# Re-cutting the first strip's output products around a batch's attention work, and moving one kv block by half a slot

## The chip, the cores and the metric

The kernel runs on one core of a Trainium2 chip. The metric is the time of one execution on the device in microseconds (us), the median of several executions. A profile is the record of one execution; times inside it count from the first recorded instruction ("span"), and the span is some 1.8 us shorter than the time. All runs here are fast ones at a granted TensorE clock of 0.998 to 1.000; the two single looks (b_again1, b_again2) have no state of their own but the same clock. Each time is compared with the kernel before in the same rounds.

## The reference

Linear attention over 8 batches, 8 heads, 576 tokens and head size 64, with a normalisation per head and token, then a bilinear feed-forward layer:

```python
kv = np.einsum('bhsd,bhse->bhde', k, v)
out = np.einsum('bhsd,bhde->bhse', q, kv)
rms = np.sqrt(np.mean(out * out, axis=-1, keepdims=True) + 1e-06)
x = out / rms * g_norm            # to 4608 tokens x 512
y = ((x @ w_a) * (x @ w_b)) @ w_out   # 512 -> 1536 -> 512
```

## The kernel before

The feed-forward layer goes over nine strips of 512 tokens. In each strip, 12 units (L161 with wa_t, wb_t) make the hidden block `ab`, and 4 groups of 12 products with wo_t make the output. A product is one matmul of the algorithm, and a bank is one of the eight parts (0 to 7) of the memory P that TensorE writes its results into. TensorE is the scarce engine (98% busy), so the attention of later batches is slipped between these products. Batch 1 is slipped between the output products of strip 0, one head pair p per step:

```python
    ffn_o(0, 0, X[0])                     # group 0: 12 products, bank 4
    pieces = [(1, h1), (1, h2), (2, h1), (2, h2), (3, h1), (3, h2)]
    for n, (g, fcs) in enumerate(pieces):
        halves[0] = n > 0                 # from n=1 each product is two 64-column halves
        o_mm(0, g, O, fcs)                # 6 products of group g into bank O = 3
        if fcs is h2:
            o_out(0, g, O)                # copy of bank 3 to SBUF (VectorE or ScalarE), store
        if 0 <= n - 2 < NP:
            A.pss(n - 2, SS)              # sums of squares (TensorE), rs = 1/sqrt (ScalarE)
            A.pst(n - 2, X[n % 2])        # xt = x * g * rs (VectorE)
        if 0 <= n - 1 < NP:
            A.x(n - 1, X[(n - 1) % 2])    # x = q @ kv; needs kvb and qT; banks 4,5 or 0,1
            A.psq(n - 1, X[(n - 1) % 2])  # square (ScalarE)
        if n < NP:
            A.qtr(n, 2)                   # q transposes into bank 2; needs the load of qt
            A.kv1(n, 2)                   # kv products into bank 2; need the loads of kt, vt
            A.kv_out(n, P[:, 2, STRIP - D :])  # kvb: two copies (ScalarE)
            A.qtr_out(n, 2)               # qT: copy (VectorE)
```

Batch 2, the third batch when counted from 1, is slipped into strip 1. `slot(A, 1, n)` is called after unit n, and with n - 0.5 between a unit's two halves. At slot `k0` all 40 kv products of the batch run, the "kv block" (its loads are `ktl` and `vtl`, issued by GpSimd behind all others; the first 8 products read only the larger load of each, from the ninth on the small second load is read too); at slot `x0` come the token products (L293), which read their result `kvs`:

```python
        k0, x0 = {1: (5, 6.5), 2: (1, 2.5), ... }[s]
        if n == k0 and s in (1, 2, 3, 5):
            ...
                for p in range(NP):
                    a.kv(p, kb[:, i, p, :])
```

Cuts in this code are marked by "..."; the comments are mine.

## Time and profile before

| | kernel before |
|---|---|
| time, first 3 runs | 312.71, 312.70, 312.86 us |
| span of the profile | 310.8 us |
| TensorE busy | 98% |
| first output product (start) | 35.15 us |
| first unit of strip 1 (start) | 49.96 us |

The timelines that carry the argument stand in the prediction. Here is one more, of the weight loads (start, length, then engine, line, operation and count, and in brackets the idle time ahead of it). It shows how the wait of the third batch's kv block looks from the other side:

```profile
60.10 0.42 PEld L178 LDWEIGHTS <-ktl 128*64 128x64 bf16 x9
60.69 0.58 PEld L178 LDWEIGHTS <-ktl 128*64 128x64 bf16 x31 [0.17 <-issue]
```

Nine weights are in, the ninth product does not start, and the next weight load comes at 60.69. The view that sums up waits has no row that names the load (it has 0.2 us of "PEld L178 <- issue"); a start-to-start comparison finds the wait.

### The profile page before, as it was taken

How to read it: one execution, taken by the hardware profiler on the slowest of the kernel's cores; microseconds unless marked ns; L12 is line 12 of the kernel's file. 1: busy time of each engine (PE TensorE's matmuls, PEld its weight loads, DVE VectorE, ACT ScalarE, POOL GpSimd, SP SyncE). 2: the span in 40 equal slices, each digit the busy share in tenths (PEclk: the TensorE clock that was granted, in tenths of full speed). 3: DMA queues.
4: the chain of work that ended last, by engine and by line, in shares of the span. 5: the costliest groups of instructions: out<-in, count | busy, mean ns of one | idle time of the engine just before them, and what ended most of it. 6: DMA issues, size and time to landing. Idle time of an engine off the chain costs nothing.

```text
span 310.8 us, 6542 instructions
## 1 busy us (share of the span) xinstructions
PE 304.3 (98%) x2684; PEld 157.6 (51%) x2701; DVE 140.6 (45%) x235; ACT 117.0 (38%) x231; POOL 101.3 (33%) x123
## 2 busy tenths in 40 slices
PE   7899999999999999999999999999999999999996
PEld 3444476655555555555555555444444444444444
DVE  4544335458248603484386123752782143214321
ACT  3743255354255313551564034632651233123310
POOL 8954991093274630043646300221240000000000
PEclk9999999999999999999999999999999999999999
DMA  8999999999899999047998990073021200030002
GB/s 180 197 196 199 201 188 168 161 169 184 174 137 185 139 174 193 2 84 134 178 177 118 162 188 2 19 160 110 20 51 42 103 1 0 34 103 0 0 36 101
DMA packets 94403, 36.29 MB, mean 117 GB/s; under 512 B 64934, under 2 KB 89894, under 8 KB 94374
## 3 DMA queue, kind: packets, MB, share of 16 engines
q0 software_dynamic: 59120, 18.44, 56.6%
q1 hardware_dynamic: 34786, 16.93, 25.0%
q10 hardware_dynamic: 468, 0.51, 0.6%
q8 instruction: 21, 0.34, 0.5%
q14 instruction: 8, 0.07, 0.1%
HBM read 37.78 MB, written 12.98 MB: 163 GB/s over the span
## 4 chain that ended last, share of the span: by engine, by line
PE 79%; DMA 12%; POOL 7%; issue 1%; ACT 0%; POOLq 0%
PE P L161 77%; DMA wb_t<-in_moe_w_b_dram 6%; DMA vtl<-in_v_dram 4%; DMA wo_t<-in_moe_w_out_dram 2%; PE P L293 1%; PE P L178 1%; POOL vt L119 1%; POOL qt L119 1%; POOL qs L142 1%; POOL kt L119 1%; POOL wa_t L477 0%; POOL wb_t L477 0%; POOL wo_t L134 0%; POOL ktl L145 0%; POOL vtl L145 0%
## 5 line engine op out<-in xcount | busy, mean ns | idle before, releaser
L377 DVE TENSOR_TENSOR ab<-P,asb 128x512 bf16<-128x512 f32 x108 | 74.4, 691 | 103.2 <-PE P L161 99.9
L161 PE MATMUL P<-xt,wb_t 128*64 128x512 bf16 (+1 forms) x641 | 111.4, 379 | 0.2
L161 PE MATMUL P<-xt,wa_t 128*64 128x512 bf16 (+1 forms) x636 | 111.0, 379 | 0.6 <-issue 0.2
L373 ACT CAST asb<-P 128x512 bf16<-128x512 f32 x108 | 63.1, 586 | 89.6 <-PE P L161 89.5
L161 PE MATMUL P<-wo_t,ab 128*64 128x512 bf16 (+3 forms) x673 | 95.5, 371 | 0.3
L161 PEld LDWEIGHTS <-ab 128*64 128x64 bf16 (+1 forms) x678 | 47.5, 106 | 45.0
L161 PEld LDWEIGHTS <-wa_t 128*64 128x64 bf16 (+1 forms) x644 | 46.0, 106 | 46.2 <-issue 0.6
L161 PEld LDWEIGHTS <-wb_t 128*64 128x64 bf16 (+1 forms) x644 | 45.8, 106 | 45.8
L330 POOL TENSOR_TENSOR sqt<-rst,g_all 128x512 f32<-128x512 f32 (+1 forms) x24 | 25.0, 1046 | 83.0 <-ACT rst L323 83.0
L429 ACT COPY osb<-P 128x512 f32<-128x512 f32 x17 | 10.0, 586 | 70.2 <-PE P L161 60.2
L431 DVE COPY osb<-P 128x512 f32<-128x512 f32 x18 | 12.4, 691 | 44.9 <-PE P L161 40.4
L142 POOL DMA_DIRECT2D qs<-in_q_dram x12 | 19.8, 1654 | 0.7 <-issue 0.3
L314 DVE TENSOR_REDUCE sst<-sqt 128x8 f32<-128x512 f32 (+1 forms) x24 | 16.3, 680 | 1.7 <-ACT sqt L310 1.5
L339 DVE TENSOR_TENSOR qv<-P,sqt 128x512 bf16<-128x512 f32 x18 | 12.3, 681 | 0.0
L330 POOL TENSOR_TENSOR k_x<-rst,g_all 128x512 f32<-128x512 f32 x6 | 6.3, 1044 | 17.4 <-ACT rst L323 17.4
L323 ACT ACTIVATE rst<-sst,eps_t 128x8 f32<-128x8 f32 (+1 forms) x30 | 9.0, 300 | 7.2 <-DVE sst L314 7.0
L310 ACT ACTIVATE sqt<-P 128x512 f32<-128x512 f32 x18 | 10.5, 585 | 0.1
L243 DVE SCALAR_TENSOR_TENSOR xt<-P,g_col,rs 128x288 bf16<-128x288 f32 x16 | 7.5, 511 | 5.1 <-ACT rs L233 5.1
L134 POOL DMA_DIRECT2D wo_t<-in_moe_w_out_dram x12 | 6.4, 530 | 6.7 <-DMA wb_t<-in_moe_w_b_dram 3.2
L233 ACT ACTIVATE rs<-P,eps_t 128x576 f32<-128x576 f32 (+1 forms) x9 | 6.1, 689 | 3.7 <-PE P L161 3.4
L139 POOL COPY gate<-qT 1x1 bf16<-1x1 bf16 x5 | 0.9, 177 | 18.9 <-DVE kvs L618 14.0
L444 PE MATMUL P<-zeros 128*128 128x512 bf16 x16 | 5.8, 510 | 1.2 <-DVE eps_t L461 1.2
(72 smaller groups left out, 131.7 us busy)
## 6 DMA issues: line engine op xcount, KB each, us to landing
out_dram<-osb SPq DMA_DIRECT2D x23, 256.0 KB, 2.1
qs<-in_q_dram POOLq DMA_DIRECT2D x12, 288.0 KB, 7.5
ktl<-in_k_dram POOLq DMA_DIRECT2D x6, 512.0 KB, 9.6
vtl<-in_v_dram POOLq DMA_DIRECT2D x6, 512.0 KB, 12.2
out_dram<-osb SPq DMA_DIRECT2D x13, 128.0 KB, 2.4
wo_t<-in_moe_w_out_dram POOLq DMA_DIRECT2D x12, 128.0 KB, 6.0
wa_t<-in_moe_w_a_dram POOLq DMA_DIRECT2D x5, 256.0 KB, 8.9
wb_t<-in_moe_w_b_dram POOLq DMA_DIRECT2D x5, 256.0 KB, 9.5
```

The source lines that it names most:

```text
L119: nc.gpsimd.dma_start(out=t[:, hs, :, :], in_=src[b, hs].rearrange("h (t c) d -> t h c d", c=EC))
L142: nc.gpsimd.dma_start(out=d[:, hs, :], in_=q[b, hs].rearrange("h t d -> t h d"))
L161: nc.tensor.matmul(o[r], lhsT=lhsT[:, r], rhs=rhs, **kw)
L310: nc.scalar.activation(sqt[c % 3][r], self.by_head(c)[r], AF.Square)
L314: nc.vector.reduce_sum(sst[c % 3][r], sqt[c % 3][r].rearrange("t j p d -> t (j p) d"), axis=mybir.AxisListType.X,)
L323: nc.scalar.activation(rst[c % 3][r], sst[c % 3][r], AF.Abs_reciprocal_sqrt, bias=eps_t[r], scale=1.0 / D,)
L330: nc.gpsimd.tensor_mul(sqt[c % 3][r].rearrange("t j p d -> t (j p) d"), rst[c % 3][r].unsqueeze(2).to_broadcast([n, H, D]), g_all[r].unsqu ...
L339: nc.vector.tensor_mul(t[r].rearrange("t (p j) d -> t j p d", j=2), self.by_head(c)[r], sqt[c % 3][r])
L373: nc.scalar.copy(self.t, self.a)
L377: nc.vector.tensor_mul(abt[self.s % 2][self.fc], self.b, self.t)
L429: nc.scalar.copy(t, P[:, i, :])
L431: nc.vector.tensor_copy(t, P[:, i, :])
```

## The change

The intent is to let the kv products of pairs 0 and 1 come later, when their loads have landed, by putting two more output products ahead of them, and to do the same to the third batch's kv block with half a slot. The second group moves to bank 1, so that the third group's first two products can follow it at once. No work is added or removed; two more products run at full width and two fewer as halves.

```diff
-    h1, h2 = range(0, FC // 2), range(FC // 2, FC)
...
-    pieces = [(1, h1), (1, h2), (2, h1), (2, h2), (3, h1), (3, h2)]
-    for n, (g, fcs) in enumerate(pieces):
+    cuts = (12, 20, 26, 32, 36, 42, 48)
+    for n, cut in enumerate(cuts[1:]):
         halves[0] = n > 0
-        o_mm(0, g, O, fcs)
-        if fcs is h2:
-            o_out(0, g, O)
+        for i in range(cuts[n], cut):
+            g, fc = divmod(i, FC)
+            bank = X[1] + 1 if g == 1 else O
+            o_mm(0, g, bank, (fc,))
+            if fc == FC - 1:
+                o_out(0, g, bank)
...
-        k0, x0 = {1: (5, 6.5), 2: (1, 2.5), 3: (4, 5.5), ...}[s]
+        k0, x0 = {1: (5.5, 6.5), 2: (1, 2.5), 3: (4, 5.5), ...}[s]
```

More of the change, by code (lines that the diff above doesn't have):

```diff
@@ L608, in slot @@
             xs = tuple(x0 + x for x in (0, 1.5, 2.5, 4, 5))
-        k0, x0 = {1: (5, 6.5), 2: (1, 2.5), 3: (4, 5.5), 4: (0, 0.5), 5: (4, 5.5), 6: (0, 0.5)}[s]
+        k0, x0 = {1: (5.5, 6.5), 2: (1, 2.5), 3: (4, 5.5), 4: (0, 0.5), 5: (4, 5.5), 6: (0, 0.5)}[s]
         if n == k0 and s in (1, 2, 3, 5):
```

## The prediction

> **What bounds the kernel now.** I read the page first, then the chain that ended last, then the TensorE timeline around the two places that the diff touches, and last the weight-load, VectorE and ScalarE timelines at the spots where TensorE started late. The page says who is the bound:
>
> ```profile
> span 310.8 us, 6542 instructions
> PE 304.3 (98%) x2684; PEld 157.6 (51%) x2701; DVE 140.6 (45%) x235; ACT 117.0 (38%) x231; POOL 101.3 (33%) x123
> ```
>
> TensorE is busy 98% of the span at a granted clock of 1.000, and neither the amount nor the shape of its work changes, so the change can only be worth TensorE's own late starts. The chain of waits names where a transfer, not TensorE, set the pace:
>
> ```profile
> 36.47 0.63 POOL vt L119
> ...
> 47.20 13.45 DMA vtl<-in_v_dram
> 60.69 0.69 PE P L178 x32
> 61.38 2.59 PE P L161 x24
> ```
>
> Columns are start, length (us), what. The chain is one row of GpSimd loads up to the load of the third batch's v (vtl), then TensorE alone to the end: after 60.69 nothing but TensorE sets the time. So a microsecond saved on TensorE after 60.69 is a microsecond off the span, and one saved before counts only if the landing at about 60.65 does not take it back. The TensorE timeline (start, length, line, operands) shows the late starts:
>
> ```profile
> 39.13 0.45 PE L202 MATMUL P<-ident,qt 96*64 96x96 bf16 x12
> 39.60 0.38 PE L178 MATMUL P<-vt,kt 96*64 96x64 bf16 x12
> ...
> 41.33 0.45 PE L202 MATMUL P<-ident,qt 96*64 96x96 bf16 x12
> 41.82 0.38 PE L178 MATMUL P<-vt,kt 96*64 96x64 bf16 x12
> ...
> 43.80 0.45 PE L202 MATMUL P<-ident,qt 96*64 96x96 bf16 x12
> 44.05 0.38 PE L178 MATMUL P<-vt,kt 96*64 96x64 bf16 x12
> ...
> 45.54 0.44 PE L161 MATMUL P<-sq,ones 128*64 128x288 bf16 x4
> 45.92 0.44 PE L161 MATMUL P<-qT,kvb 128*64 128x288 bf16 x4
> ```
>
> The lengths are modelled and overlap, so read start to start. From the q transposes (L202) to the kv products (L178) it is 0.25 us undisturbed (43.80 to 44.05), but 0.47 for head pair 0 and 0.49 for pair 1. So these kv products start 0.22 and 0.24 us late; they wait for the pair's v load (issued 34.24 and 36.47; that group lands 5.3 to 5.9 us after issue, so about 39.6 and 41.8). From the sums of squares to the x product (kvb) it is 0.24 elsewhere (43.31 to 43.55), 0.38 here: 0.14 us late. A fourth late start is the kv block of the third batch:
>
> ```profile
> 60.32 1.07 PE L178 MATMUL P<-vtl,ktl 128*64 128x64 bf16 x40
> 61.19 1.06 PE L161 MATMUL P<-xt,wa_t 128*64 128x512 bf16 x8
> ...
> 86.20 0.80 PE L178 MATMUL P<-vtl,ktl 128*64 128x64 bf16 x40
> 86.83 1.03 PE L161 MATMUL P<-xt,wa_t 128*64 128x512 bf16 x8
> ```
>
> The same 40 products take 0.63 us at 86.20 and 0.87 at 60.32, so 0.24 us is waiting for vtl's landing. All four together are 0.22 + 0.24 + 0.14 + 0.24 = 0.84 us, 0.27% of the span: the ceiling of any gain.
>
> **What the Trainium skill says.** "TensorE: Matmul & The Clock Gate", Back-to-back issue gap, gives N/2.4 + 2.5 ns for one warm matmul, 216 ns at N=512; the trace agrees (the eight halves of four 512-column products take 0.86 us, 62.06 to 62.92). Part 3 of that page says that matmuls on different column tiles run at the same time; the trace agrees: twelve half-width products took 1.30 us (39.79 to 41.09), 216 ns a pair, as one full-width product. So doing two more products at full width and two fewer in halves costs nothing. "Perfetto Trace Analysis", Tensor Engine Instruction, says a recorded start lies after the semaphores are met and the end is computed; that is why I read waits as late starts. "PSUM — Partial Sum Buffer", PSUM bank collisions, says the scheduler orders two engines that touch one bank and quadrant even at different columns; the trace agrees: VectorE's copy of qT out of bank 2 always comes after ScalarE's kvb copies out of it.
>
> **The change, part by part.** It adds and removes no work. (a) Over the first strip's remaining 36 output products the cuts move from 6,6,6,6,6,6 to 8,6,6,4,6,6. Before the transposes of pairs 0, 1 and 2 stand two more products than before (2 x 0.216 = 0.43 us), before those of pair 3 as many as before. (b) The second group accumulates in bank 1 instead of 3, so the third group's first two products need not wait for the second's copy; before, about 1.3 us of other work lay between, and no wait shows there. (c) The third batch's kv block comes after the first half of unit 6 instead of before it: 4 x 0.216 = 0.865 us later in the stream.
>
> Step by step, from 35.15 where the output products start. Pair 0's transposes move from 39.13 to 39.56, its kv to 39.81, past the landing at 39.6: **0.22 us saved**. Then 6 products (1.30), x of pair 0 (0.24), transposes (0.25): pair 1's kv is due at 39.81 + 0.19 + 1.30 + 0.24 + 0.25 = 41.79, almost exactly the landing of 41.8. So the second stall goes too, **0.24 us saved**. But both savings together are only what the two extra products cost: TensorE is at 41.8 at the same point of the pair-1 step, only two products ahead.
>
> Here is the catch. Everything that follows pair 1's kv comes at its old time: six products, the sums for pair 0 at about 43.3, and behind them this chain:
>
> ```profile
> 44.56 0.94 DVE L243 SCALAR_TENSOR_TENSOR xt<-P,g_col,rs 128x288 bf16<-128x288 f32 x2 [1.30 <-ACT rs L233]
> 45.42 0.45 DVE L209 COPY qT<-P 128x576 bf16<-128x576 bf16 x1
> 45.79 0.68 DVE L431 COPY osb<-P 128x512 f32<-128x512 f32 x1
> ```
>
> Sums (43.31) to ScalarE rs (43.78, 0.74) to VectorE's two xt products (44.56) to qT of pair 2 (45.42 to 45.87); ScalarE's kvb copies, behind rs and sq, end at the same 45.38. TensorE's x of pair 2 started at 45.92, just after qT: this is the 0.14 us stall above. In the new order TensorE reaches it with 4 products instead of 6, 0.43 us sooner, and the chain is not sooner. So I expect x of pair 2 to start at about 45.9 again, now **0.55 us late instead of 0.14**: 0.43 is given back. After it both orders have done the same work (36 products), so TensorE is where it was, at best 0.03 us ahead. **Part (a) and (b): 0.22 + 0.24 - 0.43 = 0.03 us.** Two further places are close but hold: the third group's copy, on VectorE after qT, ends at 46.47 and the fourth group needs its bank at about 46.58; x of pair 3 still has six products ahead of it.
>
> Part (c): the kv block comes at 60.29 + 0.865 = 61.15 against a landing at 60.65, half a microsecond clear: **0.24 us saved**, and nothing takes it back, as TensorE runs without a late start of this kind from there to the end (later irregular spacings are 0.10 us at each batch's token products, in both kernels, and single missing records). The first user of its result, the token products at slot 6.5, comes 0.10 us (a change of tile shape) after 1.73 us of other products; VectorE's copy (0.42 us; after the kv block it started within 0.25) is done about 1.1 us ahead, and qT's transposing transfer (issued 50.5, 11.2 us to landing, 61.7) is 2 us ahead.
>
> Sum: 0.03 + 0.24 = about 0.26 us. 312.71 - 0.26 = **312.45 us**, 0.08% faster.
>
> **Rivals.** First, that the pieces' gain survives: if x of pair 2 does not wait for qT, or the chain moves up with the rest, 0.22 + 0.24 + 0.24 = 0.70 us come off, 312.0. For it: this is plainly what the cuts are for. Against it: VectorE runs from xt to qT without a gap and TensorE starts 0.05 us after qT ends. Second, that a new wait outgrows the gain: the shortened pair-2 slot lets the third group's copy or sq of pair 1 (ended 45.06, and the sums now due at 45.09) hold TensorE, or the late kv block leaves the token products waiting for kvs. The first two would cost about 0.1 us, the third is 1.1 us off; 312.6 to 312.8. Third, that the transfers land elsewhere than in the profiled execution: loads are one row at about 200 GB/s up to 60 us, so if vtl lands 0.5 us later in unprofiled runs, moving the block saves up to 0.7 us, 312.0; if it lands 0.3 us sooner, the whole change is worth nothing, 312.7.
>
> **Range and chances.** The three runs before lie within 0.16 us, so the range is set by the rivals: 312.1 to 312.75. The whole ceiling is 0.84 us and no new wait I can name reaches 1 us, against 6.25 us for 2%: faster 0.005, same 0.99, slower 0.005.
>
> **What would show it.** Right: kv of pair 0 some 0.25 us after its transposes; pair 1's near 41.8 with at most 0.05 us of waiting; x of pair 2 near 45.9 with 0.55 us of late start behind qT; the kv block of the third batch in 0.63 us; token products near 63.65. Wrong: x of pair 2 before 45.7 (first rival), sums of pair 1 or the fourth group's first product late (second), or the block still in pieces (third).

## The result

Over six runs each the kernel before took 312.60 us (312.23 to 312.86) and the changed one 312.59 us (312.39 to 312.73). The ratio is 1.0, with a 95% interval of 0.9987 to 1.0013. A ratio is the mean time of one kernel's runs over that of the other's of the same rounds, so it is not quite the ratio of the medians quoted.

The profile of the changed kernel, in the TensorE timeline at the places shown of before:

```profile
39.60 0.45 PE L202 MATMUL P<-ident,qt 96*64 96x96 bf16 x12
39.88 0.35 PE L178 MATMUL P<-vt,kt 96*64 96x64 bf16 x12
...
41.61 0.42 PE L202 MATMUL P<-ident,qt 96*64 96x96 bf16 x12
41.87 0.35 PE L178 MATMUL P<-vt,kt 96*64 96x64 bf16 x12
...
45.15 0.42 PE L161 MATMUL P<-sq,ones 128*64 128x288 bf16 x4
45.95 0.44 PE L161 MATMUL P<-qT,kvb 128*64 128x288 bf16 x4 [0.37 <-DVE qT L209]
...
61.21 0.82 PE L178 MATMUL P<-vtl,ktl 128*64 128x64 bf16 x40
61.84 1.06 PE L161 MATMUL P<-xt,wb_t 128*64 128x512 bf16 x8
```

The three load waits are gone: 0.28 and 0.26 us from transposes to kv products, 0.63 us for the kv block. In their place x of pair 2 starts 0.80 us after its sums where 0.24 is undisturbed: 0.56 us late, behind VectorE's qT copy. VectorE's timeline is here that of before, shifted by 0.02 us:

```profile
44.58 0.94 DVE L243 SCALAR_TENSOR_TENSOR xt<-P,g_col,rs 128x288 bf16<-128x288 f32 x2 [1.30 <-ACT rs L233]
45.44 0.45 DVE L209 COPY qT<-P 128x576 bf16<-128x576 bf16 x1
45.81 0.68 DVE L431 COPY osb<-P 128x512 f32<-128x512 f32 x1
```

And the chain that ended last now passes through that copy instead of through the loads:

```profile
43.81 0.75 ACT rs L233
44.62 0.40 issue
45.02 0.51 DVE xt L243
45.52 0.38 DVE qT L209
45.95 0.44 PE P L161 x4
```

In these two profiles the first unit of strip 1 starts at 49.96 and 49.99 us (the pieces gave nothing), and from there the 0.24 us of the kv block remain: spans 310.84 and 310.62, a difference of 0.22 us where the prediction's sum is 0.26. But the medians do not show it. Either the 0.2 us is lost in the noise, or these two profiles are not what most executions look like.

### The profile page after: what moved, and what is told of

It is laid out like the page before. It is cut to its first block, busy times and chain, and to the rows that moved or that the text cites. A ratio compares the mean times of both kernels' runs of the same rounds, so it can differ in the third digit from the quotient of the medians.

```text
span 310.6 us, 6555 instructions
## 1 busy us (share of the span) xinstructions
PE 305.3 (98%) x2699; PEld 157.0 (51%) x2699; DVE 140.5 (45%) x235; ACT 117.2 (38%) x231; POOL 101.3 (33%) x123
## 4 chain that ended last, share of the span: by engine, by line
PE 95%; DMA 2%; ACT 1%; DVE 1%; issue 0%; ACTq 0%
PE P L161 91%; DMA qv<-in_v_dram 2%; PE P L178 2%; PE P L293 1%; PE P L202 1%; PE P L216 0%; DVE xt L243 0%; ACT sq L225 0%; ACT rs L233 0%; PE P L444 0%; ACT vc L497 0%; PE P L505 0%; ACTq L453 0%; DVE qT L209 0%; PE P L517 0%
## 5 line engine op out<-in xcount | busy, mean ns | idle before, releaser
L444 PE MATMUL P<-zeros 128*128 128x512 bf16 x17 | 6.6, 529 | 1.2 <-DVE eps_t L461 1.2
```

## The experiments

Theory: the cuts trade load waits for a longer wait of x of pair 2 behind VectorE's qT, and the half slot removes a real wait. Rivals: the cuts do save time; or the load waits of the one profile are no property of the kernel, so in most executions there is less to save. In what follows the **stretch** is the time from the first output product to the first unit of strip 1, and the **block** is from the first of the third batch's kv products to the next product after them. Both are read from each run's TensorE timeline.

### One part alone: the cuts (e1_cuts), the half slot (e2_half)

```diff
 # e1_cuts: the changed kernel, but
-k0, x0 = {1: (5.5, 6.5), ...
+k0, x0 = {1: (5, 6.5), ...
 # e2_half: the kernel before, but
-k0, x0 = {1: (5, 6.5), ...
+k0, x0 = {1: (5.5, 6.5), ...
```

> Cuts and bank of the change, third batch's kv block back at its old place. My theory (the pieces only trade the two load waits for a longer wait of x of pair 2 behind qT): kv of pairs 0 and 1 start 0.25 us after their transposes, x of pair 2 near 45.95 with 0.4 to 0.6 us of late start, TensorE at the first unit of strip 1 (49.96 before) within 0.05 us, the kv block again takes about 0.87 us instead of 0.63; span of before within 0.05 us, time 312.6. Rival 1 (the pieces do save time): first unit of strip 1 at 49.5, but then the kv block is due sooner and waits longer, 0.7 us, so the time is the same and only the trace tells them apart. Rival 2 (in other executions vtl lands early enough and the kv block never waits): the kv block takes 0.63 us here.

Measured: 312.69 us against 312.50 for before, ratio 1.0005 (0.9992 to 1.0018). The load waits of pairs 0 and 1 are gone, x of pair 2 is 0.56 us late, the stretch is 14.79 us, and the block waits for vtl as foreseen:

```profile
60.45 0.32 PE L178 MATMUL P<-vtl,ktl 128*64 128x64 bf16 x8
60.93 0.69 PE L178 MATMUL P<-vtl,ktl 128*64 128x64 bf16 x32 [0.16 <-DMA vtl<-in_v_dram]
61.43 1.06 PE L161 MATMUL P<-xt,wa_t 128*64 128x512 bf16 x8
```

Eight products run, then the ninth waits for the second vtl load; 61.43 - 60.45 = 0.98 us, 0.35 of it waiting. The span is 311.06 us, 0.22 over the first profile where 0.05 at most was expected: the first output product came 0.15 us later and the block waited 0.11 longer.

> Only the kv block half a slot later, old cuts and bank. My theory: both load waits (0.22 and 0.24 us) and 0.14 us behind qT stay as in the kernel before, the kv block takes 0.63 us in place of 0.87, span about 310.6, time 0.24 us under before, as the full change. Rival 1 (the cuts are what let the block move): kv block waits again though later. Rival 2 (no wait in most executions): time equal to before within 0.05 us although the profile shows the wait gone.

Measured: 312.55 us against 312.50, ratio 0.9999 (0.9987 to 1.0012). The block takes 0.63 us (61.36 to 61.99). But the load waits did not stay as in the kernel before, though its pieces are the old ones:

```profile
39.59 0.45 PE L202 MATMUL P<-ident,qt 96*64 96x96 bf16 x12
39.87 0.35 PE L178 MATMUL P<-vt,kt 96*64 96x64 bf16 x12
...
41.60 0.42 PE L202 MATMUL P<-ident,qt 96*64 96x96 bf16 x12
41.99 0.38 PE L178 MATMUL P<-vt,kt 96*64 96x64 bf16 x12
```

0.28 and 0.39 us instead of 0.47 and 0.49, and a stretch of 14.53 us instead of 14.80. In this execution TensorE came to the transposes of pair 0 at 39.59 instead of 39.13, late enough to find pair 0's load in place and to wait only 0.14 us for pair 1's. The time, 0.05 us over before, is the one that rival 2 expected. This is the first sign of the second rival: the old order has less to wait for when TensorE happens to be late, and the new order pays its 0.56 us regardless.

### Moving the short slot (e3_six) and keeping the lead (e4_fill)

```diff
 # e3_six: the changed kernel, but
-cuts = (12, 20, 26, 32, 36, 42, 48)
+cuts = (12, 20, 26, 32, 38, 42, 48)
 # e4_fill: cuts = (12, 20, 26, 32, 38, 44, 48), and the last sums come inside unit 0:
+u0.mm(wa_t, (0, 1, 2)); A.pss(3, SS); A.pst(3, X[1]); u0.mm(wb_t, (0, 1, 2))
```

> The changed kernel with cuts 8,6,6,6,4,6: the short slot moves from the step that waits for x of pair 2 to the next. My theory (the time of x of pair 2 is set by the VectorE chain xt, qT): x of pair 2 starts at 45.95 as in the changed kernel, but late by only 0.12 to 0.15 us since two more products stand before it; x of pair 3 then starts near 48.18, now 0.4 us late, because its own chain is no sooner; total equal to the changed kernel within 0.05 us. Rival (x of pair 2 waits for something that comes after the products, so its lateness is a fixed cost of 0.56 us): x of pair 2 near 46.4 and the time 0.4 us over the changed kernel. Rival (the lateness vanishes and nothing takes it back): 0.4 us under the changed kernel.

> The two products ahead are kept all the way (cuts 8,6,6,6,6,4), and the sums of pair 3 come after the first three products of unit 0, so that TensorE has ready work while the chain runs. My theory: x of pair 2 and x of pair 3 start at 45.95 and 48.18 as in the changed kernel with two more products done before each (late by 0.15 at most), the first unit of strip 1 begins near 49.3 in place of 49.99, its last products (kc 3) are then held only by xt of pair 3 near 52.2 (52.57 before); net 0.3 us under the changed kernel, 312.3 on the scale where before is 312.6. Rival (bank 3 and ScalarE's copy of the last output group hold unit 0): 0.1 us or less under the changed kernel. Rival (kv block now comes before vtl lands): its 40 products take over 0.63 us.

Measured: 313.92 us (ratio 1.0042, 1.0029 to 1.0056) and 313.95 us (1.0043, 1.0031 to 1.0055). Both expectations missed, because I had overlooked a wait of my own making. Product 36 is the first of group 3; with a cut at 38 it follows group 2 directly in the same bank 3:

```profile
44.54 1.03 PE L161 MATMUL P<-wo_t,ab 128*64 128x512 bf16 x8
46.80 0.62 PE L161 MATMUL P<-wo_t,ab 128*64 128x512 bf16 x4 [1.23 <-DVE osb L431]
```

This is e3_six: four products of group 2, then 1.40 us of nothing (46.80 less 44.54 and 4 x 0.216). VectorE's copy out of bank 3 stood behind its xt and qT work (46.07 to 46.75 in this run), and the next product into the bank starts at 46.80. e4_fill shows the same gap. So by their times the two runs do not decide what they were made for. One part of e3_six's theory can still be read: x of pair 3, which now follows the short slot, is 0.56 us late behind qT,

```profile
49.04 0.44 PE L161 MATMUL P<-sq,ones 128*64 128x288 bf16 x4
49.84 0.44 PE L161 MATMUL P<-qT,kvb 128*64 128x288 bf16 x4 [0.37 <-DVE qT L209]
```

while in e4_fill, with six products in that slot, it is 0.15 us late (49.27 to 49.66). The late start goes where the short slot goes. The two runs also show why the changed kernel's short slot is where it is: the cut at 36 is the group boundary, and the sums, x, transposes and kv products that follow it hide the handover of bank 3. No other bank is free at that step: 0 and 1 hold x of pair 1, 4 and 5 receive x of pair 2, 2 holds the transposes, 6 and 7 the sums.

### TensorE made late on purpose (d_old, d_new)

```diff
 # d_old: the kernel before; d_new: the changed kernel; both with
+dummy(2, 7)          # two idle 512-column products, 0.43 us
 ffn_o(0, 0, X[0])
```

> The kernel before with two idle products (0.43 us of TensorE) put in front of the first strip's output products. Theory A (in the old order the load waits of pairs 0 and 1 absorb a TensorE that comes later, in the new order nothing does): the 0.43 us is mostly absorbed, both kv blocks start 0.25 to 0.30 us after their transposes, x of pair 2 is late by 0.14 as before, and the kv block of the third batch waits as before; time 0 to 0.15 us over before. Theory B (no load wait to speak of in most executions): 0.4 us over before.

> The changed kernel with the same two idle products. Theory A (the wait of x of pair 2 is a chain that starts at the kv product of the step before, so it moves with TensorE): nothing is absorbed, x of pair 2 is late by 0.56 again but at 46.4, first unit of strip 1 at 50.4; time 0.43 us over the changed kernel, 0.3 to 0.45 over d_old plus or minus the 0.24 that the kv block saves. Theory B (x of pair 2 waits for a fixed time set by loads): x of pair 2 at 45.95 still, late by 0.13 only, time equal to the changed kernel.

Measured: 312.88 us (ratio 1.0011, 0.9999 to 1.0024) and 313.02 us (1.0017, 1.0003 to 1.0031), with before at 312.47. The stretch, which begins after the idle products, is 14.53 us in d_old and 14.79 in d_new. In d_old (old order) kv starts at most 0.28 us after the transposes for both pairs, so a late TensorE no longer waits for loads. In d_new x of pair 2 moved with TensorE:

```profile
45.89 0.42 PE L161 MATMUL P<-sq,ones 128*64 128x288 bf16 x4
46.69 0.44 PE L161 MATMUL P<-qT,kvb 128*64 128x288 bf16 x4 [0.37 <-DVE qT L209]
```

0.80 us after its sums again, and 0.74 us later than in the changed kernel, just as its first output product is (35.93 against 35.19). So the new wait is no fixed time that a late TensorE runs out: it is a chain that starts at TensorE's own earlier products and keeps its 0.56 us. Theory A holds for the mechanism. Its numbers for d_old do not: the block took 0.63 us instead of waiting, and instead of 0 to 0.15 us the median rose by 0.41. That rise does not tell how much load wait most executions hold, for d_old's profile has two waits that the theory left out: 0.15 us at the first product of group 2 (0.34 us after the kv products, 42.01 to 42.35, where 0.19 is undisturbed; explained under b_again1) and 0.14 us at the first product of strip 2 (traced under e9_new). The medians of d_new and d_old differ by 0.14 us, less than their intervals.

### The kernel before again (b_again1, b_again2)

No edit.

> The kernel before, unchanged, profiled a second time. Theory A: what its kv products wait for the loads is no property of the kernel but of where the loads and TensorE happen to stand in one execution, so the stretch from the first output product to the first unit of strip 1 is between 14.45 and 14.81 us (14.80 in the first profile) and equal to 14.39 us plus the load waits; the kv block of the third batch takes between 0.63 and 1.0 us. Theory B (the first profile is typical): 14.80 and 0.87 again within 0.03.

> The kernel before, unchanged, profiled a third time. As for b_again1: theory A 14.45 to 14.81 us and 0.63 to 1.0 us, differing from the other two profiles by over 0.05 us in at least one of the two; theory B 14.80 and 0.87.

Measured: 312.50 and 312.20 us, single runs. They were run on another chip. Stretch 14.53 and 14.68 us, block 0.63 us in both. The kernel before did not wait for vtl at all in these two executions. Theory B is wrong. Theory A's ranges hold, but not its sum: 14.39 us plus load waits gives 14.42 for b_again1. The TensorE timeline of b_again1:

```profile
39.54 0.45 PE L202 MATMUL P<-ident,qt 96*64 96x96 bf16 x12
39.82 0.35 PE L178 MATMUL P<-vt,kt 96*64 96x64 bf16 x12
...
41.81 0.35 PE L178 MATMUL P<-vt,kt 96*64 96x64 bf16 x12
42.15 1.49 PE L161 MATMUL P<-wo_t,ab 128*64 128x512 bf16 x12
...
60.45 0.82 PE L178 MATMUL P<-vtl,ktl 128*64 128x64 bf16 x40
61.08 1.06 PE L161 MATMUL P<-xt,wa_t 128*64 128x512 bf16 x8
```

Here TensorE reached the transposes of pair 0 at 39.54, 0.41 us later than in the first profile. In its place another small wait appears: kv products take 0.19 us, but the next product starts 0.34 us after them. It is the first of group 2, and it waits for ScalarE's copy of group 1 out of bank 3:

```profile
41.52 0.58 ACT L429 COPY osb<-P 128x512 f32<-128x512 f32 x1 [0.86 <-PE P L161]
```

It ends at 42.10; the product starts at 42.15. That wait of 0.15 us is what the change's move to bank 1 takes away, and in the first profile it hid behind the load waits. Set side by side (us; late starts read as in the prediction, those of 0.03 us or less left out):

| profile | order of the pieces | first output product | late starts in the pieces | stretch | block |
|---|---|---|---|---|---|
| before, first | old | 35.15 | 0.22 + 0.24 + 0.14 | 14.80 | 0.87 |
| b_again2 | old | 35.11 | 0.10 + 0.24 + 0.14 | 14.68 | 0.63 |
| b_again1 | old | 35.56 | 0.15 + 0.14 | 14.53 | 0.63 |
| e2_half | old | 35.61 | 0.14 + 0.15 | 14.53 | 0.63 |
| changed | new | 35.19 | 0.56 | 14.79 | 0.63 |
| e1_cuts | new | 35.30 | 0.56 | 14.79 | 0.98 |

Stretch less late starts is 14.20 to 14.24 us in every row, so the account is complete to 0.04 us. Stretch plus block is 15.67, 15.31 and 15.16 us in the three profiles of the kernel before, 15.38 on average, and 15.42 in the changed kernel. The first profile, on which the prediction rests, was the slowest of the three here.

That these are waits for loads can be read from the landings in the traces. The v loads of pairs 0 and 1 landed at 39.56 and 41.78 in the first profile and at 39.40 and 41.62 in b_again2, and the kv products started 0.04 us after each; in b_again1 they had landed (39.46, 41.68) before the kv products were due. The second vtl load landed at 60.65, 60.07 and 60.09 us (first, b_again2, b_again1). It is not the chip alone that differs: b_again1 and b_again2 ran on the same chip and wait differently, and on the other chip that load landed at 60.89 in e1_cuts and at 59.42 in d_old.

### The block half a slot earlier (e5_early)

```diff
 # the kernel before, but
-k0, x0 = {1: (5, 6.5), ...
+k0, x0 = {1: (4.5, 6.5), ...
```

> The kernel before with the third batch's kv block half a slot earlier (in unit 5) instead of later. My theory (the block is held by the landing of vtl, at 59.4 to 60.9 in the profiles so far): TensorE reaches it 0.865 us sooner, near 59.5, and waits until the landing, 0.3 to 1.3 us; all of that is lost: time 0.3 to 0.9 us over before. Rival (the 40 products are slow at that place for another reason than the landing): the block takes 0.87 us again and the time is that of before.

Measured: 313.45 us, ratio 1.0028 (1.0013 to 1.0043). It was run on another chip. TensorE was held twice, once before the first product and once before the ninth:

```profile
58.54 1.06 PE L161 MATMUL P<-xt,wa_t 128*64 128x512 bf16 x8
59.65 0.32 PE L178 MATMUL P<-vtl,ktl 128*64 128x64 bf16 x8
60.39 0.70 PE L178 MATMUL P<-vtl,ktl 128*64 128x64 bf16 x32 [0.42 <-DMA vtl<-in_v_dram]
60.89 1.06 PE L161 MATMUL P<-xt,wb_t 128*64 128x512 bf16 x8
```

59.65 is 0.25 us after the last eight halves (58.54 + 0.86), and the block takes 1.24 us where 0.63 would do: together 0.86 us, and the medians rose by 0.85 (312.60 to 313.45). So the landing of vtl is a wall: all of the 0.865 us by which the block came sooner was lost in waiting for it. The half slot of the change is a safeguard against this wall, though in two of three executions the old place already cleared it.

### The bank of the second group (e6_onebank)

```diff
 # the changed kernel, but
-bank = X[1] + 1 if g == 1 else O
+bank = O
```

> The changed kernel with the second group back in bank 3, so that the third group's first two products follow the second group's last one in the same bank. My theory (a bank is handed over only after ScalarE's copy out of it): the third group's first product starts 0.8 us late (0.23 to the copy, 0.59 the copy); this moves pair 1 and its chain too, x of pair 2 is late by 0.56 again, time 0.8 us over the changed kernel. Rival (slack elsewhere takes it up): under 0.3 us over the changed kernel.

Measured: 313.52 us, ratio 1.0028 to before (1.0011 to 1.0045). It was run on another chip.

```profile
40.45 1.03 PE L161 MATMUL P<-wo_t,ab 128*64 128x512 bf16 x8
42.16 0.62 PE L161 MATMUL P<-wo_t,ab 128*64 128x512 bf16 x4 [0.68 <-ACT osb L429]
```

TensorE stands still for 0.85 us (42.16 less 40.45 and 4 x 0.216) behind ScalarE's copy of group 1, and the stretch 15.65 us against 14.79. Without the bank, the new cuts would cost 0.86 us.

### Shortening the chain (e9_new, e10_old)

```diff
 # the loop of the pieces, of the changed kernel (e9_new), or of the kernel before with k0 = 5.5 (e10_old)
+kb1 = X[(n - 1) % 2]            # free columns of the x bank
-A.kv1(n, 2); A.kv_out(n, P[:, 2, STRIP - D :])
+A.kv1(n, kb1); A.kv_out(n, P[:, kb1, STRIP - D :])
 # psq(n - 1) comes after kv1(n), and pst(n - 2) last, behind qtr_out(n)
```

> The changed kernel with kv of each pair accumulated in the free columns of the x bank in place of the transposes' bank, so that VectorE's qT copy need not wait for ScalarE's kvb copies of the same bank, and qT emitted ahead of xt on VectorE. My theory of the chain (rs, xt, qT, x): qT of pair 2 starts near 44.3 in place of 45.44, xt of pair 0 follows, x of pair 2 starts near 45.65 instead of 45.95, late by 0.25 in place of 0.56; first unit of strip 1 near 49.7; time 0.3 us under the changed kernel. Rival (x of pair 2 is held by ScalarE's kvb copies, which stay behind rs and sq): x of pair 2 at 45.5 to 45.95 and the qT copy early with no effect: 0 to 0.1 us.

> Old cuts and bank, kv block half a slot later, and the same split of banks as e9_new. My theory: x of pair 2 no longer late (0.14 us saved), load waits of pairs 0 and 1 as far as TensorE is early (0 to 0.46 us, as in the kernel before), kv block 0.63 us: from the first output product to the first unit of strip 1 14.25 to 14.7 us, against 14.80 in the changed kernel and 14.53 to 14.81 with the old order; time 0.1 to 0.35 us under before, 312.2 to 312.4.

Measured: 312.41 us (312.09 to 313.20; ratio 1.0001, 0.9988 to 1.0013) and 312.50 us (1.0002, 0.9989 to 1.0014). In e9_new the qT copy no longer waits for ScalarE's copies out of the same bank, nor stands behind xt on VectorE (the edit removes both links at once, so it does not tell which of the two held it; in the changed kernel both ended within 0.12 us of each other, 45.41 and 45.52):

```profile
44.35 0.46 DVE L209 COPY qT<-P 128x576 bf16<-128x576 bf16 x1 [1.77 <-PE P L202]
44.73 0.93 DVE L243 SCALAR_TENSOR_TENSOR xt<-P,g_col,rs 128x288 bf16<-128x288 f32 x2
```

It starts 1.09 us sooner than in the changed kernel, and TensorE follows:

```profile
45.24 0.44 PE L161 MATMUL P<-sq,ones 128*64 128x288 bf16 x4
45.49 0.54 PE L161 MATMUL P<-qT,kvb 128*64 128x288 bf16 x4
45.84 0.45 PE L202 MATMUL P<-ident,qt 96*64 96x96 bf16 x12
46.24 0.38 PE L178 MATMUL P<-vt,kt 96*64 96x64 bf16 x12
```

x of pair 2 starts 0.25 us after its sums, no longer late, although ScalarE's kvb copies came 0.11 us later than in the changed kernel (45.09 against 44.98). This shows that the chain through qT was what held x of pair 2, and not the kvb copies. The stretch is 14.54 us, 0.25 less and not 0.56, because other waits took over: above all, the kv products of pair 3 start 0.15 us late, 0.04 us after their v load landed (46.20).

The span is 310.64 against 310.62 all the same: TensorE then stood still for 0.21 us in front of the first product of strip 2 (82.54). The trace tells what for. Ahead of that product the weight-load queue waits for the semaphore of the third transposing transfer of batch 2's tokens, issued at 76.69; its last count came at 82.40, 5.7 us after the issue, and the weights followed at 82.51. In d_old the same transfer took 5.6 us, to 82.84, and the product came at 82.98; in the changed kernel and the kernel before it took 4.2 and 4.1 us and held nothing. Why it took longer in those two runs is open. In e10_old x of pair 2 is no longer late at all, and the two load waits take 0.18 and 0.24 us; stretch 14.67. Neither version beats the kernel before beyond the noise.

## Why the prediction was right, and where not

The median of 312.59 us lies within the stated range, 0.14 over the number, and "within 2%" came true. That the total fits is partly luck: the forecast gain of 0.26 us does not show in the medians (312.60 to 312.59), and the range was wide enough to hold no change at all. The mechanism, read from the traces, fared better than the sum. Point by point:

- **Ceiling of 0.84 us, no change of clock or amount of work:** nothing contradicts them.
- **Load waits of pairs 0 and 1 vanish, pair 1's kv near 41.8:** held (0.28 and 0.26 us after the transposes, 41.87).
- **The saving is given back at x of pair 2, near 45.9, 0.55 us late behind qT:** held (45.95, 0.56). e9_new confirms the cause by shortening that chain.
- **The kv block in 0.63 us:** held; e1_cuts and e5_early confirm that it is the landing of vtl that it clears.
- **The two close places (group 3's bank, x of pair 3):** held in the changed kernel; e3_six shows what the first costs when it does not hold.
- **The step that failed** is the sum, "0.03 + 0.24 = about 0.26 us", in its terms for the kernel before. The terms 0.22, 0.24 and 0.24 were read from one profile and taken as the kernel's own. In two further profiles of the same kernel they were 0.10, 0.24, 0 and 0.03, 0.01, 0, while the 0.56 us on the side of the change stayed in each of three profiles (changed, e1_cuts, d_new). So the cuts are not worth 0.03 us but between 0.01 and -0.26 (14.80, 14.68, 14.53 less 14.79), and the half slot between 0 and 0.24. On the average of the three profiles the sum is -0.04 us instead of 0.26. The prediction named this as its third rival ("if it lands 0.3 us sooner, the whole change is worth nothing"; vtl landed 0.56 and 0.58 us sooner in the two further profiles), but it gave no weight to it in its sum and looked only at vtl, not at TensorE's own arrival, which varied by half a microsecond (35.11 to 35.61).
- **"(b) ... no wait shows there":** true of that profile only. When TensorE comes late, the old order waits 0.15 us for bank 3 (b_again1).
- **"Loads are one row at about 200 GB/s up to 60 us":** misread. The page of the kernel before has 188 GB/s from 39 to 47 us, 168 and then 161 from there to 62.

Not settled: why TensorE's arrival and the landings differ from one execution to the next, how often each case occurs (three profiles of the kernel before are few), and whether the change is worth plus or minus 0.1 us on average. The interval of the ratio, some 0.4 us to each side, is wider than that.

## What to carry to other kernels

A wait for a load seen in one profile is the difference of two times that both move from one execution to the next; before counting it as a gain, look whether it is still there in a second and third profile of the same kernel, because work moved to cover it may cost a fixed amount every time. When products are moved ahead of a wait, follow the next chain between engines that starts behind it: if that chain begins at the delayed instruction, the moved products are only waited out later. And a cut between accumulation groups needs other work behind it or another bank: the handover of one bank through a copy cost 0.15 to 1.40 us here.

## What the Trainium skill lacked or had wrong

- "TensorE: Matmul & The Clock Gate", Back-to-back issue gap, gives about 131 ns per matmul as the sustained figure for N=512 and calls the 216 ns of its formula too high there. Here the sustained pace was the formula's: 200 half-width products, two at a time, took 21.70 us in the chain of the kernel before, 217 ns a pair, with a weight load before each; 104 full-width products of the changed kernel took 22.55 us, 217 ns each.
- "DMA: Bandwidth & Descriptors", Anatomy of one DMA, gives a fit for one DMA (2.0 us plus bytes over 436 GB/s), but I found nothing in it on a queue full of loads or on the spread between executions. The 64 KB second load of vtl, which an estimate from the fit puts at about 2.15 us, landed 13.4 us after issue in the first profile of the kernel before, 13.0 in b_again1 and 12.1 in d_old.
- None of the pages that I read says that a gap behind a load may be there in one execution and absent in the next. Here the same kernel's kv block took 0.87, 0.63 and 0.63 us in three profiles, and its pieces 14.80, 14.68 and 14.53 us.
